# Token blocks in groups of one, two and three: a new order for attention steps and experts on one core

## The chip, the cores and the metric

The kernel runs on one core of one Trainium2 chip. The metric is device time in microseconds of that core, the median of several runs; it was 943.03 us over three runs (942.54 to 943.67).

The profile names the engines PE (matrix multiply, with its weight loads as PEld), DVE (vector), ACT (scalar activation), POOL (GpSimd) and SP (here the issuer of every DMA). Each engine takes its instructions in the order in which the program lists them, and semaphores order them across engines.

## The reference

A recurrence with a decaying state is followed by a dense mixture of four experts. Cut to what is computed:

```python
# B, H, S, D = 4, 8, 768, 48
for t in range(S):
    cur = einsum('bhd,bhe->bhde', u * k[t], v[t])
    y[t] = einsum('bhd,bhde->bhe', r[t], state + cur)
    state = w[t][..., None] * state + einsum('bhd,bhe->bhde', k[t], v[t])
x = y as (N, DM)                      # N = B*S = 3072 tokens, DM = H*D = 384
p = probs / (probs.sum(-1) + 1e-9)
for e in range(4):                    # w1[e]: 384 x 1024, w2[e]: 1024 x 384
    out += p[:, e:e+1] * (relu(x @ w1[e]) @ w2[e])
```

## The kernel before

**Units and blocks.** The sequence is cut into chunks of C = 128 steps. One batch of one chunk is an attention *unit* n (24 in all; chunk n // 4, batch n % 4). The four units of a chunk make one token *block* of 512 tokens for the experts (six blocks, 0 to 5).

**Attention.** A unit is computed in chunked form. Its parts are: `decays` (two scans on DVE that make the running decay products g and e), `scale` (r times e and k times g, on DVE), `own_product` and `own_score` (the token's own term with u: products on POOL, a reduction dg on DVE, then a diagonal a on POOL or ACT), `scores` (PE: sc, then a transpose kt; DVE copies the masked sc into a), `values` (PE: yp; ACT and DVE split it in a high part and a rest into the expert input x), `fill` (two DMAs move 16 rows of x), `carry` (PE: up; updates the state) and `guard` (ACT: tests that the decays are in range; it overwrites wx). Four steps make a unit go on: `step_a(n)` is decays(n+1) and scores(n), `step_b(n)` is scale(n+1) and own_score(n+1), `step_c(n)` is values(n), fill(n) and guard(n+1), `step_d(n)` is carry(n). `go()` takes the next step of a list; a step_c of chunk 3 or later waits in that list until an x buffer is free (three buffers). On PE a step_a shows as sc and kt, a step_c as yp, a step_d as up; step_b has no matmul.

**Experts.** For one block and one expert, a *turn*: eight f1 products (`f1`, tile pf1, two PSUM buffers; nine 128x512 matmuls each: x and w1 are split in a high part and a rest, and three products are kept), each read by ACT (relu, hh) and then by DVE (the rest, hl); then four f2 products (`f2`, tile pf2, 24 matmuls of 128x384 each, one for each batch). Weights come in quarters: `load_w` fetches a quarter into one of four raw buffers, `split_w` makes the high part on ACT and the rest with two subtractions on POOL or DVE, so eight quarters make an expert.

**Order.** All engines' lists follow the order in which the code is written. Blocks are taken in pairs: twelve passes (three pairs by four experts, the order of experts reversed from pair to pair so that one expert's weights are kept at each boundary). After each f1, and twice in each f2, `go()` takes one attention step, so a turn has 16 such gaps. In the first pass block 0 runs in two halves (SEG = 2, 2: f1 matmuls are 128x256, and each f2 has four gaps), so that it can start when two units are done. `upto(n)` takes all steps that a block needs before it starts.

**Start.** Units 0 and 1 are written out ahead of the loop, through a loop body with two rounds. `warm_up` issues matmuls on a zero tile between their parts (FILL = 12, 4, 4, 8). `setup_c` normalizes the probabilities on DVE just before the first f1.

Of the kernel before, what the change touches and what calls it, by code (L numbers as in the profile page):

```python
# [21 lines left out]
NCH = S // C  # L22
# [13 lines left out]
NRAW, XB, PB, WARM = 4, 3, 2, 12  # L36
SEG = (2, 2)
FILL = (12, 4, 4, 8)
# [3 lines left out]
def chunked_path(ctx, tc, dmaj, tmaj, u_bc, probs, w1, w2, out, flag):  # L42
# [11 lines left out]
    p_acc = pool("acc", PB)  # L54
# [122 lines left out]
    def own_score(n, diag=True):  # L177
# [4 lines left out]
        if diag:  # L182
            own_diag(n)

    def own_diag(n):
        s = un[n]
        dg = s["dg"]
# [11 lines left out]
    def decays(n):  # L199
        s = un[n]  # L200
        wx, c, b = s["wx"], s["c"], s["b"]
        g = p_one.tile([ROWS, WLEN], F32, name="g", tag="g")
        e = p_one.tile([ROWS, WLEN - 1], F32, name="e", tag="e")
        nc.vector.tensor_tensor_scan(g[:, WLEN - 1:0:-1], wx[:, WLEN - 1:0:-1], ones1[:, WLEN - 1:0:-1],  # L204
                                     0.0, ALU.mult, ALU.add)
        gv = g[:, 1:].rearrange("p (i t) -> p i t", i=NP)
# [153 lines left out]
    for sb in range(NCH // PB):  # L360
        passes += [(sb, e) for e in order]
        order = order[::-1]
    fresh = [i for i, (sb, e) in enumerate(passes) if i == 0 or passes[i - 1][1] != e]
# [71 lines left out]
    def turn(pi, e, blk, first, last, b0, nb, before, after):  # L435
        for f in range(FT):
            before(f)
            f1(e, blk, f, b0 * C, nb * C)
            after(f)
            go()  # L440
        for b in range(b0, b0 + nb):
            f2(e, blk, b, first, last, go, 4 if pi == 0 and blk == 0 else 2)

    with tc.manual_schedule():
        act_table()
        setup_a()
        for what in ("w", "k", "r"):
            load(0, what)
        nc.sync.dma_start(out=u_sb, in_=u_bc)
        for what in ("own", "v"):  # L450
            load(0, what)
        warm_up(FILL[0])
        for what in ("w", "k", "r", "own", "v"):
# [5 lines left out]
        setup_b()  # L459
        decays(0)  # L460
        guard(0)
        load(2, "w")
        scale(0)
        own_product(0)
        own_score(0)
        nc.sync.dma_start(out=pr, in_=probs)
        decays(1)
        for n in range(SEG[0]):
            scores(n)
            guard(n + 1)  # L470
            load(n + 2, "k")
            load(n + 2, "r")
            if n == 0:
                own_product(n + 1)
                own_score(n + 1, False)
            scale(n + 1)
            if n > 0:
                own_product(n + 1)
            else:
                own_diag(n + 1)  # L480
            warm_up(FILL[1])
            values(n)
            fill(n)
            if n > 0:
                own_score(n + 1)
            else:
                decays(n + 2)
            load(n + 2, "own")
            split_next((0, 1, n), n == 0)
            carry(n)  # L490
            load(n + 2, "v")
            warm_up(FILL[2])
            del un[n], steps[-4:]
            load(n + 3, "w")
        warm_up(FILL[3])
        setup_c()
        for pi, (sb, e) in enumerate(passes):
            first, last = pi % NE == 0, pi % NE == NE - 1
            for bi in range(PB):
                blk = sb * PB + bi  # L500
                next_w1 = bi == PB - 1 and pi + 1 in fresh
                own_w2 = bi == 0 and pi in fresh

                def before(f):
                    pass

                def after(f):
                    if f % 2 == 1 and next_w1:
                        split_next((passes[pi + 1][1], 1, f // 2), True)
                    if pi == 0 and bi == 0 and b0 == 0 and f % 2 == 0 and (0, 1, f // 2 + 1) in raw_t:  # L510
                        split_next((0, 1, f // 2 + 1), f % 4 == 0)
                    if f % 2 == 1 and own_w2 and b0 == 0:
                        split_next((e, 2, f // 2), pi > 0 or f % 4 == 1)
                    if f == FT - 1 and last:
                        read.add(blk)

                b0 = 0
                for nb in SEG if pi == 0 and bi == 0 else (B,):
                    if first:
                        upto(blk * B + b0 + nb - 1)  # L520
                    turn(pi, e, blk, first, last, b0, nb, before, after)
                    b0 += nb

# [189 lines left out]
```

## Time and profile before

| | us |
|---|---|
| median of three runs | 943.03 |
| the profiled execution | 942.2 |
| its span, first to last instruction | 940.4 |
| PE busy | 917.8 |
| DVE busy | 373.7 |
| POOL busy | 281.6 |
| ACT busy | 251.7 |

The profiled execution's time is 1.8 us more than its span, and 0.8 us under the median. Matmuls are pipelined and their ends are modelled, so a busy PE isn't PE at its peak: a turn's real length is read from where its first matmul starts to where the next turn's first starts. First f1 matmuls of before's turns start at 29.64 (block 0, first half), 73.71 (second half), 112.41 (block 1), 156.64 and 189.67.

### The profile page before, as it was taken

The page shows a single profiled execution, that of the slowest core. Times are in us where ns is not written, and L with a number is a line of the kernel's source. Part 1 is how long each engine was busy: PE and PEld are TensorE (multiplying, and loading weights), DVE is VectorE, ACT ScalarE, POOL GpSimd, SP SyncE. Part 2 cuts the span into 40 slices and gives each one's busy share as a digit, 9 for nine tenths or more (in the row PEclk, how much of TensorE's full clock was granted, in tenths as well). Part 3 has the DMA queues.
Part 4 walks back from the last instruction along what each step waited for, and adds up shares of the span by engine and source line. Part 5 has one row for each costly group of instructions (what it writes and reads, how often), then busy time and mean ns, then how long its engine had stood idle before and what let it go on. Part 6 is the DMA issues. An engine that isn't in the chain of part 4 may idle for free.

```text
span 940.4 us, 13744 instructions
## 1 busy us (share of the span) xinstructions
PE 917.8 (98%) x5629; PEld 818.1 (87%) x5629; DVE 373.7 (40%) x573; ACT 251.7 (27%) x454; POOL 281.6 (30%) x279
## 2 busy tenths in 40 slices
PE   6889999999999999999999999999999999999997
PEld 5778879989998978898998899898998899899887
DVE  8998793222122677742112212273202212222221
ACT  3434352231132232223213212412113312311310
POOL 5665583231132334323113213340003212311300
PEclk8999999999999999999999999999999999999999
DMA  8563542220121433331012112230102112101001
GB/s 251 173 195 119 169 151 78 68 64 22 51 68 34 143 118 117 106 93 53 32 51 68 34 34 68 61 105 10 51 1 68 35 35 68 52 33 51 9 26 37
DMA packets 34536, 70.49 MB, mean 75 GB/s; under 512 B 4512, under 2 KB 13088, under 8 KB 34464
## 3 DMA queue, kind: packets, MB, share of 16 engines
q1 hardware_dynamic: 34464, 69.52, 23.8%
q8 instruction: 46, 0.75, 0.3%
q14 instruction: 26, 0.21, 0.1%
HBM read 62.43 MB, written 4.72 MB: 71 GB/s over the span
## 4 chain that ended last, share of the span: by engine, by line
PE 91%; DVE 2%; issue 2%; DMA 1%; ACT 0%; SPq 0%; DVEq 0%
PE pf L343 42%; PE pf L323 41%; PE yp L257 2%; PE sc L230 2%; PE yp L252 2%; PE up L286 1%; DMA r<-in_dmaj 1%; PE kt L236 1%; DVE a L238 0%; DVE g L204 0%; DVE w1l L139 0%; DVE k L222 0%; DVE r L221 0%; DVE hl L330 0%; DVE zst L209 0%
## 5 line engine op out<-in xcount | busy, mean ns | idle before, releaser
L323 PE MATMUL pf<-x,w1h 128*128 128x512 f32 (+1 forms) x1200 | 362.7, 385 | 1.3 <-DMA x<-y 1.3
L330 DVE SCALAR_TENSOR_TENSOR hl<-pf,hh 128x512 fp32r<-128x512 f32 (+1 forms) x200 | 133.6, 668 | 321.8 <-ACT hh L329 321.7
L323 PEld LDWEIGHTS pf<-x,w1h 128*128 128x128 f32 x1200 | 221.0, 189 | 46.0 <-issue 2.7
L343 PE MATMUL pf<-w2h,hh 128*128 128x384 f32 x768 | 260.0, 339 | 0.0
L343 PE MATMUL pf<-w2h,hl 128*128 128x384 f32 x768 | 257.2, 335 | 0.0
L343 PE MATMUL pf<-w2l,hh 128*128 128x384 f32 x768 | 256.8, 334 | 0.0
L329 ACT ACTIVATE hh<-pf 128x512 fp32r<-128x512 f32 (+1 forms) x200 | 116.2, 581 | 459.6 <-PE pf L323 458.8
L323 PE MATMUL pf<-x,w1l 128*128 128x512 f32 (+1 forms) x600 | 229.2, 382 | 0.5 <-POOL w1l L139 0.5
L139 POOL TENSOR_TENSOR w1l<-raw,w1h 128x384 fp32r<-128x384 f32 x76 | 79.1, 1062 | 255.8 <-ACT w1h L134 255.8
L343 PEld LDWEIGHTS pf<-w2h,hh 128*128 128x128 f32 x768 | 144.2, 188 | 3.3 <-issue 1.7
L343 PEld LDWEIGHTS pf<-w2l,hh 128*128 128x128 f32 x768 | 144.2, 188 | 0.7
L343 PEld LDWEIGHTS pf<-w2h,hl 128*128 128x128 f32 x768 | 144.2, 188 | 0.3 <-DVE hl L330 0.3
L139 POOL TENSOR_TENSOR w2l<-raw,w2h 128x384 fp32r<-128x384 f32 x76 | 76.6, 1029 | 219.9 <-ACT w2h L134 217.7
L323 PEld LDWEIGHTS pf<-x,w1l 128*128 128x128 f32 x600 | 113.2, 189 | 22.5 <-POOL w1l L139 0.7
L352 DVE SCALAR_TENSOR_TENSOR acc<-pf,pr,acc 128x384 f32<-128x384 f32 x72 | 44.4, 616 | 215.6 <-PE pf L343 215.6
L195 POOL TENSOR_TENSOR a<-ident,dg 128x512 f32<-128x512 f32 x47 | 50.4, 1093 | 52.6 <-DVE dg L181 48.2
L211 DVE TENSOR_TENSOR_SCAN e<-wx,zst 112x516 f32<-112x516 f32 x24 | 50.3, 2095 | 0.8
L257 PE MATMUL yp<-a,v 128*64 128x128 f32 (+1 forms) x384 | 32.3, 296 | 11.8 <-DVE a L238 9.7
L257 PEld LDWEIGHTS yp<-a,v 128*64 128x64 f32 (+1 forms) x384 | 23.8, 138 | 18.8 <-DVE a L238 14.6
L175 POOL TENSOR_TENSOR rkt<-rkt,u_sb 128x384 f32<-128x384 f32 x22 | 37.8, 1719 | 1.7
L134 ACT CAST w1h<-raw 128x768 fp32r<-128x768 f32 x40 | 33.1, 828 | 0.0
L134 ACT CAST w2h<-raw 128x768 fp32r<-128x768 f32 x40 | 33.1, 827 | 0.0
(66 smaller groups left out, 444.1 us busy)
## 6 DMA issues: line engine op xcount, KB each, us to landing
raw<-in_w SPq DMA_DIRECT2D x80, 384.0 KB, 3.0
rkt<-in_tmaj SPq DMA_DIRECT2D x23, 384.0 KB, 3.4
wx<-in_dmaj SPq DMA_DIRECT2D x24, 226.2 KB, 3.2
k<-in_dmaj SPq DMA_DIRECT2D x24, 224.0 KB, 2.9
r<-in_dmaj SPq DMA_DIRECT2D x24, 224.0 KB, 4.0
v<-in_tmaj SPq DMA_DIRECT2D x24, 192.0 KB, 3.2
out<-acc SPq DMA_DIRECT2D x24, 192.0 KB, 1.9
x<-y SPq DMA_DIRECT2D x48, 48.0 KB, 3.0
```

The lines of the kernel that those rows point to most:

```text
L134: nc.scalar.copy(hi, t)
L139: eng.tensor_tensor(lo[:, s], t[:, s], hi[:, s].bitcast(F32), ALU.subtract)
L175: eng.tensor_tensor(s["rt"], s["rt"], u_sb, ALU.mult)
L195: nc.gpsimd.tensor_tensor(a, ident.unsqueeze(1).to_broadcast([128, NP, C]), dg[:, q].unsqueeze(2).to_broadcast([128, NP, C]), ALU.mult)
L211: nc.vector.tensor_tensor_scan(e, wx[:, 0:WLEN - 1], zst.rearrange("p i t -> p (i t)"), 0.0, ALU.mult, ALU.add)
L230: nc.tensor.matmul(sc[j][:, i, :], s["kk"][half(j), i, :], s["rr"][half(j), i, :], start=True, stop=True)
L257: nc.tensor.matmul(y[wide(j), i, :], v[:, h * D:h * D + (64 if j == 0 else D)], s["a"][j][:, i, :], start=(c == 0 and i == 0), stop=(i == ...
L323: nc.tensor.matmul(p[:, 0:nt], wv[:, k, fs], x[:, k, bs, i, :], start=(k == 0 and n == 0), stop=(k == KT - 1 and n == 2))
L329: nc.scalar.activation(hh[:, ts], p[:, 0:nt], AF.Relu)
L330: nc.vector.scalar_tensor_tensor(hl[:, ts], p[:, 0:nt], 0.0, hh[:, ts].bitcast(F32), ALU.max, ALU.subtract)
L343: nc.tensor.matmul(p, hv[:, ts], wv[:, o, :], start=(f == 0 and n == 0), stop=(f == FT - 1 and n == 2))
L352: nc.vector.scalar_tensor_tensor(a[:, b, :], p, sc, a[:, b, :], ALU.mult, ALU.add)
```

## The change

Four things change.

- **Groups.** Instead of three pairs, blocks go through the four experts as (0,), (1, 2), (3, 4, 5). There are still twelve passes and ten loads of an expert. Splits of w2 now follow the first four f1 of a pass's first turn, splits of the next expert's w1 the last four f1 of its last turn; in the group of one both fall in the same turn, eight splits in eight f1. A third `acc` buffer is added.
- **Pace.** `gap()` takes the place of `go()`: each gap adds a credit (0.5; 0.3 in the second half of block 0; 0.75 for blocks 3 to 5), and a step is taken for each full credit. In a normal turn of 16 gaps that is 8 or 12 steps, not 16.
- **Start.** Units 0 and 1 are written in another order. `decays` is cut in two, `after_decays` (g) and `until_decays` (the reciprocal and e); unit 1's g alone stands ahead of unit 0's masked copy. own_product(0) moves from DVE to POOL. r and k of unit 0 are loaded after u and the own-term rows. guard(0) moves behind scores(0), and wx of unit 2, whose buffer it frees, with it. All four w1 quarters of expert 0 are split before the first f1. The last warm-up shrinks from 4 + 8 to 4 matmuls.
- **Diagonals.** For both units 0 and 1 the second diagonal is made on ACT.

```diff
-NRAW, XB, PB, WARM = 4, 3, 2, 12
+NRAW, XB = 4, 3
+GROUPS = ((0,), (1, 2), (3, 4, 5))
 SEG = (2, 2)
-FILL = (12, 4, 4, 8)
+FILL = (12, 4, 4, 4)
...
-    p_acc = pool("acc", PB)
+    p_acc = pool("acc", max(len(g) for g in GROUPS))
...
-        eng = nc.vector if n == 0 else nc.gpsimd
-        eng.tensor_tensor(s["rt"], s["rt"], s["kt"], ALU.mult)
-        eng.tensor_tensor(s["rt"], s["rt"], u_sb, ALU.mult)
+        nc.gpsimd.tensor_tensor(s["rt"], s["rt"], s["kt"], ALU.mult)
+        nc.gpsimd.tensor_tensor(s["rt"], s["rt"], u_sb, ALU.mult)
...
-            if n == 0 and q == 1:
+            if n < SEG[0] and q == 1:
...
+    def after_decays(n):
+        s = un[n]
+        wx = s["wx"]
+        g = s["g"] = p_one.tile([ROWS, WLEN], F32, name="g", tag="g")
         nc.vector.tensor_tensor_scan(g[:, WLEN - 1:0:-1], wx[:, WLEN - 1:0:-1], ones1[:, WLEN - 1:0:-1],
                                      0.0, ALU.mult, ALU.add)
...
+    pace, credit = [0.5], [0.0]
+
+    def gap():
+        credit[0] += pace[0]
+        while credit[0] >= 1:
+            credit[0] -= 1
+            go()
...
-            before(f)
             f1(e, blk, f, b0 * C, nb * C)
             after(f)
-            go()
+            gap()
         for b in range(b0, b0 + nb):
-            f2(e, blk, b, first, last, go, 4 if pi == 0 and blk == 0 else 2)
+            f2(e, blk, b, first, last, gap, 8 // nb)
...
         decays(0)
-        guard(0)
-        load(2, "w")
-        scale(0)
         own_product(0)
+        scale(0)
         own_score(0)
-        nc.sync.dma_start(out=pr, in_=probs)
-        decays(1)
...
+        after_decays(1)
+        scores(0)
+        load(2, "k")
+        guard(0)
+        load(2, "w")
+        load(2, "own")
+        until_decays(1)
+        scale(1)
+        own_product(1)
+        warm_up(FILL[1])
+        values(0)
...
+        for blk in g:
+                segs = SEG if pi == 0 else (B,)
+                    next_w1 = blk == g[-1] and pi + 1 in fresh and b0 + nb == B
+                    own_w2 = blk == g[0] and pi in fresh and b0 == 0
+                    if pi == 0:
+                        pace[0] = 0.5 if b0 == 0 else 0.3
+                    elif blk >= GROUPS[-1][0]:
+                        pace[0] = 0.75
+                    else:
+                        pace[0] = 0.5
...
+                        if own_w2 and f < NQ:
+                            split_next((e, 2, f), pi > 0 or f % 2 == 1)
+                        if next_w1 and f >= FT - NQ:
+                            split_next((passes[pi + 1][1], 1, f - FT + NQ), True)
```

Three places show how the order moves. In the lists pf is a PSUM tile of f1, hl its second reader on DVE, and a number after a name only tells one buffer from another.

The first is DVE in a full-size turn with attention steps in its f1 phase, from the hl of the first f1 on. Before (block 1, first pass):

```order
L330 SCALAR_TENSOR_TENSOR hl<-pf_1388,hh 128x512
L204 SCALAR_TENSOR_TENSOR g<-wx,ones_100 112x516
L209 TENSOR_SCALAR zst<-g 112x4
L210 RECIPROCAL zst<-zst 112x4
L211 SCALAR_TENSOR_TENSOR e<-wx,zst 112x516
L238 COPY_PREDICATED a_1327<-mask,sc_1409 128x512
L238 COPY_PREDICATED a_1329<-mask,sc_1410 128x512
L330 SCALAR_TENSOR_TENSOR hl<-pf_1432,hh 128x512
L221 TENSOR_TENSOR r<-r,e 112x512
L222 TENSOR_TENSOR k<-k,g 112x512
L181 TENSOR_REDUCE dg<-rkt 128x8
L330 SCALAR_TENSOR_TENSOR hl<-pf_1463,hh 128x512
```

Now (block 0, second expert), the same engine and place:

```order
L334 SCALAR_TENSOR_TENSOR hl<-pf_994,hh 128x512
L203 SCALAR_TENSOR_TENSOR g<-wx,ones_100 112x516
L213 TENSOR_SCALAR zst<-g 112x4
L214 RECIPROCAL zst<-zst 112x4
L215 SCALAR_TENSOR_TENSOR e<-wx,zst 112x516
L242 COPY_PREDICATED a_874<-mask,sc_1022 128x512
L242 COPY_PREDICATED a_876<-mask,sc_1023 128x512
L334 SCALAR_TENSOR_TENSOR hl<-pf_1045,hh 128x512
L334 SCALAR_TENSOR_TENSOR hl<-pf_1066,hh 128x512
L225 TENSOR_TENSOR r<-r,e 112x512
L226 TENSOR_TENSOR k<-k,g 112x512
L183 TENSOR_REDUCE dg<-rkt 128x8
```

The hl of the second f1 stands behind the whole of step_a in both; what moved is step_b, which now comes one f1 later.

The second place is PE in the same turns, from the last matmuls of the third f1 on. Before, the yp matmuls of step_c (sixteen rows, of which the first stand here) follow the third f1, and the fourth f1 comes after them:

```order
L323 MATMUL pf_1463<-x,w1h 128x512 x2
L323 MATMUL pf_1463<-x,w1l 128x512
L252 MATMUL yp<-r,sd_112 64x128
L252 MATMUL yp<-r,sd_112 48x128
L252 MATMUL yp<-r,sd_112 64x128
```

Now the fourth f1 (pf_1097) follows at once. It takes the PSUM buffer of the second (pf_1045):

```order
L327 MATMUL pf_1066<-x,w1h 128x512 x2
L327 MATMUL pf_1066<-x,w1l 128x512
L327 MATMUL pf_1097<-x,w1h 128x512 x2
L327 MATMUL pf_1097<-x,w1l 128x512
L327 MATMUL pf_1097<-x,w1h 128x512 x2
```

The yp moved two f1 further on, behind the fifth.

The third place is DVE at the start, from the reduction of unit 0's own term (dg) on. Before:

```order
L181 TENSOR_REDUCE dg<-rkt 128x8
L204 SCALAR_TENSOR_TENSOR g<-wx,ones_100 112x516
L209 TENSOR_SCALAR zst<-g 112x4
L210 RECIPROCAL zst<-zst 112x4
L211 SCALAR_TENSOR_TENSOR e<-wx,zst 112x516
L238 COPY_PREDICATED a_192<-mask,sc_206 128x512
L238 COPY_PREDICATED a_194<-mask,sc_207 128x512
```

Now:

```order
L183 TENSOR_REDUCE dg<-rkt 128x8
L203 SCALAR_TENSOR_TENSOR g<-wx,ones_100 112x516
L242 COPY_PREDICATED a_188<-mask,sc_197 128x512
L242 COPY_PREDICATED a_190<-mask,sc_198 128x512
L213 TENSOR_SCALAR zst<-g 112x4
L214 RECIPROCAL zst<-zst 112x4
L215 SCALAR_TENSOR_TENSOR e<-wx,zst 112x516
```

The two masked copies of unit 0 moved ahead of unit 1's reciprocal and second scan.

More of the change, by code (lines that the diff above doesn't have):

```diff
@@ L172, in own_product, with own_score @@
         s = un[n]
[L173 to L177 removed]
+        nc.gpsimd.tensor_tensor(s["rt"], s["rt"], s["kt"], ALU.mult)
+        nc.gpsimd.tensor_tensor(s["rt"], s["rt"], u_sb, ALU.mult)
+    def own_score(n):
         s = un[n]
@@ L359, in chunked_path @@
     passes, order = [], list(range(NE))
-    for sb in range(NCH // PB):
-        passes += [(sb, e) for e in order]
+    for g in GROUPS:
+        passes += [(g, e) for e in order]
         order = order[::-1]
-    fresh = [i for i, (sb, e) in enumerate(passes) if i == 0 or passes[i - 1][1] != e]
+    fresh = [i for i, (g, e) in enumerate(passes) if i == 0 or passes[i - 1][1] != e]
     def step_a(n):
@@ L433, in split_next, with turn @@
         owed.append(key)
-    def turn(pi, e, blk, first, last, b0, nb, before, after):
+    pace, credit = [0.5], [0.0]
[4 more added lines that the diff above has]
+            go()
+    def turn(e, blk, first, last, b0, nb, after):
         for f in range(FT):
-            before(f)
             f1(e, blk, f, b0 * C, nb * C)
             after(f)
-            go()
+            gap()
         for b in range(b0, b0 + nb):
-            f2(e, blk, b, first, last, go, 4 if pi == 0 and blk == 0 else 2)
+            f2(e, blk, b, first, last, gap, 8 // nb)
     with tc.manual_schedule():
@@ L446, in chunked_path @@
         setup_a()
-        for what in ("w", "k", "r"):
-            load(0, what)
+        load(0, "w")
         nc.sync.dma_start(out=u_sb, in_=u_bc)
-        for what in ("own", "v"):
+        for what in ("own", "r", "k", "v"):
             load(0, what)
         warm_up(FILL[0])
-        for what in ("w", "k", "r", "own", "v"):
+        for what in ("w", "r", "k", "own", "v"):
             if what == "own":
@@ L460, in chunked_path @@
         decays(0)
+        own_product(0)
+        scale(0)
+        own_score(0)
+        after_decays(1)
+        scores(0)
+        load(2, "k")
         guard(0)
         load(2, "w")
-        scale(0)
-        own_product(0)
-        own_score(0)
-        nc.sync.dma_start(out=pr, in_=probs)
-        decays(1)
[L468 to L494, printed above, removed]
+        load(2, "own")
@@ new lines, in chunked_path @@
+        until_decays(1)
[3 more added lines that the diff above has]
+        values(0)
+        load(2, "r")
+        fill(0)
+        split_next((0, 1, 0), True)
+        own_score(1)
+        carry(0)
+        load(2, "v")
+        after_decays(2)
+        scores(1)
+        load(3, "k")
+        guard(1)
+        load(3, "w")
+        split_next((0, 1, 1), True)
+        until_decays(2)
+        warm_up(FILL[2])
+        values(1)
+        load(3, "r")
+        fill(1)
@@ L495, in chunked_path @@
+        nc.sync.dma_start(out=pr, in_=probs)
+        split_next((0, 1, 2), False)
+        own_product(2)
+        scale(2)
+        carry(1)
+        load(3, "v")
+        split_next((0, 1, 3), True)
+        own_score(2)
+        load(3, "own")
+        guard(2)
+        load(4, "w")
         warm_up(FILL[3])
+        del un[0], un[1], steps[-8:]
         setup_c()
-        for pi, (sb, e) in enumerate(passes):
+        for pi, (g, e) in enumerate(passes):
             first, last = pi % NE == 0, pi % NE == NE - 1
[L499 to L515, printed above, removed]
-                b0 = 0
-                for nb in SEG if pi == 0 and bi == 0 else (B,):
@@ L519, in chunked_path @@
                     if first:
                         upto(blk * B + b0 + nb - 1)
-                    turn(pi, e, blk, first, last, b0, nb, before, after)
+                    turn(e, blk, first, last, b0, nb, after)
                     b0 += nb
```

17 lines of the change are left out of this document (9 added, 8 removed).

## The prediction

> **What bounds the kernel now.** I read the page first, then the span by stages, then the start and one turn in order of time.
>
> ```profile
> span 940.4 us, 13744 instructions
> PE 917.8 (98%) x5629; PEld 818.1 (87%) x5629; DVE 373.7 (40%) x573; ACT 251.7 (27%) x454; POOL 281.6 (30%) x279
> PE   6889999999999999999999999999999999999997
> DVE  8998793222122677742112212273202212222221
> PE 91%; DVE 2%; issue 2%; DMA 1%; ACT 0%; SPq 0%; DVEq 0%
> PE pf L343 42%; PE pf L323 41%; PE yp L257 2%; PE sc L230 2%; PE yp L252 2%; PE up L286 1%; DMA r<-in_dmaj 1%; PE kt L236 1%; DVE a L238 0%; DVE g L204 0%; DVE w1l L139 0%; DVE k L222 0%; DVE r L221 0%; DVE hl L330 0%; DVE zst L209 0%
> ```
>
> PE carries the chain (91%). It has holes only in the first slices of 23.5 us, where DVE is at eight to nine tenths; later PE is full whatever DVE does, and where DVE works hard (attention) its order must be such that PE never waits for it. By stages (columns: PE, PEld, DVE, ACT, POOL busy, clock, DMA share, GB/s):
>
> ```profile
> 29.64:73.71 44.07, 38.20 (x361) 32.57 (x361) 41.22 (x64) 18.11 (x40) 30.00 (x26) 0.92 0.59 182
> 73.71:112.41 38.70, 37.02 (x395) 31.75 (x393) 34.01 (x56) 14.28 (x35) 21.14 (x21) 1.00 0.47 142
> 156.64:189.67 33.03, 33.03 (x170) 30.18 (x169) 7.38 (x11) 8.26 (x13) 7.93 (x8) 1.00 0.14 48
> 333.34:385.28 51.94, 51.94 (x443) 43.72 (x441) 38.03 (x61) 15.27 (x32) 21.38 (x21) 1.00 0.41 123
> ```
>
> A bare turn takes 33.03 us; by the chain's 42% (L343) half of it, 16.5, is f2. The turn at 333.34 holds four attention units: (51.94 - 33.03) / 4 = 4.73 us of PE time a unit, with no hole. The two halves of block 0's first turn hold four units each and take 82.77 us. A half f1 is nine matmuls, three in 0.36 us:
>
> ```profile
> 33.14 0.40 PE L323 MATMUL pf<-x,w1h 128*128 128x256 f32 x2
> 33.50 0.40 PE L323 MATMUL pf<-x,w1h 128*128 128x256 f32 x2
> ```
>
> So 1.08, and 16 x 1.08 + 16.5 and eight units at 4.73 make 71.6: 11 us of PE time are lost there, and 29.64 pass before it. All that the change can win lies in these 41 us; the matmuls that remain are the same, apart from twelve warm-ups.
>
> **The start.** Rows of before in order of time:
>
> ```profile
> 6.66 0.72 ACT L297 ACTIVATE wx<-wx,mid 112x512 f32<-112x512 f32 x1 [4.36 <-DVE e L211]
> 7.21 0.68 DVE L222 TENSOR_TENSOR k<-k,g 112x512 f32<-112x512 f32 x1
> 10.43 0.33 SPq L153 DMA_DIRECT2D wx<-in_dmaj  x1
> 13.10 1.32 DVE L238 COPY_PREDICATED a<-mask,sc 128x512 f32<-128x512 uint32 x2
> 18.44 1.40 DVE L204 TENSOR_TENSOR_SCAN g<-wx,ones 112x516 f32<-112x516 f32 x1
> 22.61 1.30 DVE L238 COPY_PREDICATED a<-mask,sc 128x512 f32<-128x512 uint32 x2
> 25.33 3.02 PE L105 MATMUL pf<-zero 128*128 128x512 f32 x12
> 25.97 0.55 DVE L267 TENSOR_TENSOR x<-yp,x 112x384 fp32r<-112x384 f32 x1
> 26.58 1.20 SPq L274 DMA_DIRECT2D x<-y  x2
> 29.64 0.47 PE L323 MATMUL pf<-x,w1h 128*128 128x256 f32 x2 [1.29 <-DMA x<-y]
> ```
>
> DVE is the path: copy of unit 0 at 13.10, of unit 1 at 22.61, x done at 26.52, and 3.1 us later (two DMAs) f1. Unit 0: r and k come later (u and the own rows go first, 0.58 MB, some 2 us at this stage's rate), so I put the end of scale(0) at 8.6, not 7.89. The product on POOL gives the diagonal at about 11, and since e of unit 1 (2.3 us with its reciprocal) no longer stands ahead, the copy comes at 11.2, 1.9 earlier. Unit 1: its copy loses its predecessor's e too (18.44 + 1.40 to 22.61 is 2.8), but g of unit 2 must still run first, and its wx is requested later: guard(0), at 6.66 before, now stands behind the diagonals and ks on ACT and ends near 12.9, so this DMA goes out 2.5 us later and SP holds what is queued behind it (own rows, r, the fill). I put its landing at 18.7, the copy at 20.0, x at 24.0 and the first f1 at 27.1: 2.5 us won. Bounds: 25 (wx lands as before) and 29.
>
> The warm-ups at the end were twelve of 0.25; with four PE idles from about 24.0 to 27.1. What that does to the clock:
>
> ```profile
> 19.84:23.25 3.41, 2.17 (x20) 1.00 0.68 218
> 26.66:30.08 3.42, 2.13 (x12) 1.00 0.38 102
> 33.50:36.91 3.41, 1.46 (x13) 1.00 0.60 184
> 36.91:40.32 3.41, 3.32 (x21) 0.50 0.02 5
> ```
>
> (PE busy, clock, DMA.) A window of 3.41 us with 2.13 or 2.17 us of work leaves the next at full clock; one with 1.46 is followed by a window at half. So f1 will start at half clock, 1.5 us lost. It stays hidden: DVE still has a split, scale(2), dg and setup_c to do until about 29.5 and sets the pace.
>
> **First half of block 0.** Before, the f1 phase stalls like this:
>
> ```profile
> 35.88 1.31 DVE L238 COPY_PREDICATED a<-mask,sc 128x512 f32<-128x512 uint32 x2
> 36.69 2.50 PE L257 MATMUL yp<-a,v 128*64 128x128 f32 x16 [1.95 <-ACT w1h L134]
> 37.09 0.40 DVE L330 SCALAR_TENSOR_TENSOR hl<-pf,hh 128x256 fp32r<-128x256 f32 x1
> ```
>
> PE waits 1.95 for the copy, and hl, which must free a PSUM buffer, comes after it. Half a quarter's split on DVE, by the groups of lines:
>
> ```profile
> L139 DVE TENSOR_TENSOR w2l<-raw,w2h 128x384 fp32r<-128x384 f32 x4 | 2.0, 548 | 0.3 <-ACT w2h L134 0.3
> ```
>
> The new order keeps one unit instead of two in these eight f1, with step_a behind the second. DVE from 29.5: hl (0.4), a w2 quarter (2 x 0.55), hl, decays(3) with two copies (6.0, between the 5.19 and 6.60 of rows below), hl: 37.8. The fifth f1 waits for that hl; PE was done at about 34.3 (27.1, four f1, sc and kt, half clock), 3.5 us lost. Then split, hl, scale(3), dg and two hl put the seventh at 43.2 and the end of f1 at 46.0. f2 with unit 3: 8.3 + 3.7 (4.73 without the state product, the 1.08 of L252 below) = 58.0. The second half needs x of unit 3, whose yp is only two gaps before: yp ends 54.9, x 56.6, DMAs 3.1: 59.7, 1.7 lost (before, those units were done long ahead). Second half: 8.6 + 8.3 of matmuls, unit 4 with 4.7, a like stall of 3.0 (5.2 to 6.6 of DVE and 0.8 of hh and hl against two f1 and sc with kt, 3.7), ends 84.3; one half-clock window, 1.7, makes 86.0. Before stands at 112.41 with ten units; now five are done, and 112.41 - 5 x 4.73 = 88.8. **Term: -2.8**, bounds -7 (f1 at 25, stalls as short as the 1.95) and +1 (f1 at 29, DVE beside a busy POOL).
>
> **The pace.** Moved units cost 4.73 as before where nothing waits; grouping itself adds no matmul and no load (twelve passes, ten experts either way), the third acc buffer nothing. In a full-size turn before:
>
> ```profile
> 114.67 1.16 PE L230 MATMUL sc<-r,k 48*128 48x128 f32 x16
> 115.40 0.69 DVE L330 SCALAR_TENSOR_TENSOR hl<-pf,hh 128x512 fp32r<-128x512 f32 x1 [2.52 <-ACT hh L329]
> 116.01 1.22 DVE L204 TENSOR_TENSOR_SCAN g<-wx,ones 112x516 f32<-112x516 f32 x1
> 119.87 1.33 DVE L238 COPY_PREDICATED a<-mask,sc 128x512 f32<-128x512 uint32 x2
> 120.41 1.08 PE L252 MATMUL yp<-r,sd 48*64 48x128 f32 x16
> 121.09 0.67 DVE L330 SCALAR_TENSOR_TENSOR hl<-pf,hh 128x512 fp32r<-128x512 f32 x1
> 122.44 0.73 PE L323 MATMUL pf<-x,w1h 128*128 128x512 f32 x2
> ```
>
> After sc, PE runs two f1 until 120.41. The second-next hl on DVE (121.09) stands behind decays and copies and ends at 121.76; it frees the buffer of the fourth f1. Before, yp fills 120.41 to 122.44, so nobody waits. Now, at half a step a gap, the fourth f1 comes straight after the third and must wait from 120.41 to 121.76: **1.35 us** a unit. The order shows eight full-size f1 phases with a step_a, decays behind it and three f1 in a row: the turns of experts 2, 3 and 4 on block 0, both blocks of the pass after, block 1 of the next, block 2 in that group's last, and block 3's first. In four of these (the three on block 0, and block 1's second pass) POOL splits w2 quarters in the same f1. What that does to DVE:
>
> ```profile
> 139.15 2.89 POOL L139 TENSOR_TENSOR w1l<-raw,w1h 128x384 fp32r<-128x384 f32 x2
> 139.23 2.02 DVE L204 TENSOR_TENSOR_SCAN g<-wx,ones 112x516 f32<-112x516 f32 x1
> 144.50 1.33 DVE L238 COPY_PREDICATED a<-mask,sc 128x512 f32<-128x512 uint32 x2
> ```
>
> From g to the last copy 6.60 instead of 5.19, so the wait would be 2.76. POOL starts later against g here (after ACT's cast), so I take the middle of 1.35 and 2.76, 2.05. Terms: 4 x 1.35 = **+5.4**, 4 x 2.05 = **+8.2** (bounds 5.4 and 11.0).
>
> A hole of 2.05 can leave a 3.41 us window with 1.36 of work, under the 1.46 that was followed by half clock; where the window's edge cuts the hole it won't. Half of the four: 2 x 1.7 = **+3.4** (bounds 0 and 6 x 1.7 = 10). A step_a in an f2 phase needs no hl and costs nothing. Eight splits in one turn are up to 8 x 2.89 = 23 us of POOL, beside a unit's own work, in an f1 phase of some 22: POOL ends late, but each half's next use is an f1 or f2 phase away, 16.5 us, so nothing.
>
> The Trainium skill, "TensorE: Matmul & The Clock Gate", under "Why this matters for your kernels", says that PE falls back to half rate after an idle gap of more than about 3 us, one idle window. By that rule no hole of 2.76 throttles and the sum would lack the 3.4. The trace disagrees: 33.50:36.91 had 1.46 us of work, and the next window ran at 0.50; the case without half clocks is a rival below, worked out from rows.
>
> **Sum**, against the profiled execution (942.2): -2.8 + 5.4 + 8.2 + 3.4 = +14.2, 956.4. The median of the runs is 0.8 above that execution: 957.
>
> **Rivals.**
> - *Faster.* The start and the first half are worth more than I give, and the fourth f1 does not wait. For it: 13 us of holes and 29.64 of start are there, and half the DVE load of the first f1 phase goes. Point of decision: the eight waits must come to under 2.8 us, 0.35 each; or the start must gain 14. With no wait 942.2 - 2.8 = 939.4, at the best start 935: 936 to 940 on the median's scale. Against it: hl stands behind the copies in the list, and the copy's end is in the rows. Chance 0.13.
> - *No half clock* in the holes: 957.2 - 3.4 = 953.8. For it: 2.13 us of work was enough. Against: 1.46 wasn't. Chance 0.25.
> - *The weights come late.* In the group of one a raw buffer is asked for again only when POOL is done with it, SP holds later loads behind that request, and an ACT cast that waits holds relu. With 3 us and a half-clock window in each of three turns: 957 + 3 x 4.7 = 971. Against: POOL's lag is about 3 us and each quarter is asked for three splits ahead. Chance 0.10.
> - *About as before*, where start and waits cancel: 0.05, 941 to 945.
>
> My forecast proper, with two to six half windows: 0.47, its own range 948 to 965. Within 0.2% (941.1 to 944.9) is about what a measurement of this kernel can tell from no change. Faster 0.13, same 0.05, slower 0.82. Leaving out the faster case and half of the late weights: 943 to 968.
>
> **What would show it.** First f1 near 27 with a half-clock window there; copies of units 0 and 1 near 11 and 20; a hole before the fifth half f1; the second half's first f1 waiting for the DMA of x; in the turns of block 0 a PE wait of 1.4 to 2.8 at the fourth f1 after each sc, released by hl, with the clock line below 9 somewhere between 100 and 300; bare turns still 33.03. I am wrong if PE shows no wait there, or if f1 starts before 25.

## The result and the profile after

The changed kernel takes 955.88 us (median of four runs, 955.75 to 955.96), the kernel before took 943.07 beside it on the same chip. The ratio is 1.0136 with a 95% interval of 1.0118 to 1.0153: slower by 12.8 us, where 957.0 was forecast. The profiled execution has a span of 954.2, before's had 940.4: 13.8 us more.

The first lines of the page of the changed kernel, and its chain by engine:

```profile
span 954.2 us, 13657 instructions
...
PE 917.4 (96%) x5617; PEld 815.8 (85%) x5617; DVE 377.0 (40%) x569; ACT 253.6 (27%) x458; POOL 293.4 (31%) x282
...
PE   6698999999999999999999999999999999999997
...
PE 90%; DVE 4%; issue 3%; DMA 1%; ACT 1%; SPq 0%; POOL 0%; DVEq 0%
```

PE has the same busy time as before (917.4 against 917.8), so the lost time is idle time of PE. DVE's share of the chain has doubled (2% to 4%), with one and the same load (377.0 against 373.7). The digit 9 hides all of this: a tenth of a slice is 2.4 us. What PE waited for says it (engine, line, what released it; total, times, longest), first up to 110 us, then from there to 960:

```profile
PE pf L327 <- DVE hl L334: 7.0, 4, 2.7
...
PE pf L327 <- DMA pr<-in_probs: 4.3, 1, 4.3
PE pf L327 <- DMA x<-y: 2.1, 1, 2.1
```
```profile
PE pf L327 <- DVE hl L334: 9.1, 7, 1.7
```

The 4.3 and the 2.1 are the first f1 of the two halves, which wait for x. The first is put down to the load of the probabilities, which no f1 reads; it stands right behind the two DMAs of x in the queue. After 110 us one kind of wait is left in the whole kernel, seven times: an f1 (pf) that waits for an hl. An eighth stands at 99.03, in the first full turn. Its place, in order of time:

```profile
91.74 1.16 PE L234 MATMUL sc<-r,k 48*128 48x128 f32 x16
...
93.09 1.22 DVE L203 TENSOR_TENSOR_SCAN g<-wx,ones 112x516 f32<-112x516 f32 x1
...
94.34 0.80 DVE L213 TENSOR_SCALAR zst<-g 112x4 f32<-112x4 f32 x1
...
95.40 1.78 DVE L215 TENSOR_TENSOR_SCAN e<-wx,zst 112x516 f32<-112x516 f32 x1
...
97.10 1.30 DVE L242 COPY_PREDICATED a<-mask,sc 128x512 f32<-128x512 uint32 x2
...
98.31 1.27 DVE L334 SCALAR_TENSOR_TENSOR hl<-pf,hh 128x512 fp32r<-128x512 f32 x2
...
99.03 0.73 PE L327 MATMUL pf<-x,w1h 128*128 128x512 f32 x2 [1.48 <-DVE hl L334]
...
103.33 1.08 PE L256 MATMUL yp<-r,sd 48*64 48x128 f32 x16
```

This is the forecast hole: decays and copies on DVE, two hl behind them, and the fourth f1 of the turn waiting 1.48 us for the first of the two; yp, which covered the place before, now comes at 103.33. By stages (columns as in the prediction):

```profile
30.83:63.50 32.67, 27.61 (x225) 25.13 (x225) 23.58 (x40) 12.77 (x28) 18.59 (x16) 0.90 0.54 164
63.50:89.57 26.07, 23.59 (x189) 22.18 (x190) 12.38 (x20) 9.02 (x19) 13.93 (x13) 0.93 0.42 123
89.57:133.80 44.23, 42.75 (x306) 36.84 (x305) 25.04 (x35) 16.40 (x29) 29.06 (x26) 1.00 0.44 138
350.70:383.73 33.03, 33.03 (x170) 30.18 (x170) 8.00 (x12) 7.68 (x12) 7.96 (x8) 1.00 0.16 48
```

With five units done, the changed kernel stands at 89.57; before stands at 88.8 by the prediction's count: 0.8 lost in the early part. From there to the end it takes 954.2 - 89.57 = 864.6, before 828.0 (940.4 - 112.41) and five units of 4.73, 851.6: 13.0 lost in the later part. A bare turn is still 33.03.

### The profile page after: what moved, and what is told of

Its sections match the earlier page's. It is cut to its first block, busy times and chain, and to the rows that moved or that the text cites. A ratio compares the mean times of both kernels' runs of the same rounds, so it can differ in the third digit from the quotient of the medians.

```text
span 954.2 us, 13657 instructions
## 1 busy us (share of the span) xinstructions
PE 917.4 (96%) x5617; PEld 815.8 (85%) x5617; DVE 377.0 (40%) x569; ACT 253.6 (27%) x458; POOL 293.4 (31%) x282
## 4 chain that ended last, share of the span: by engine, by line
PE 90%; DVE 4%; issue 3%; DMA 1%; ACT 1%; SPq 0%; POOL 0%; DVEq 0%
PE pf L347 42%; PE pf L327 39%; PE yp L261 3%; PE yp L256 2%; PE sc L234 2%; DVE a L242 1%; PE up L290 1%; PE kt L240 1%; DVE g L203 1%; DVE hl L334 1%; DMA k<-in_dmaj 1%; ACT hh L333 0%; DMA pr<-in_probs 0%; DMA x<-y 0%; DVE e L215 0%
## 5 line engine op out<-in xcount | busy, mean ns | idle before, releaser
L327 PE MATMUL pf<-x,w1h 128*128 128x512 f32 (+1 forms) x1200 | 366.4, 388 | 22.4 <-DVE hl L334 16.1
L142 POOL TENSOR_TENSOR w1l<-raw,w1h 128x384 fp32r<-128x384 f32 x78 | 82.5, 1082 | 242.9 <-ACT w1h L137 242.1
L142 POOL TENSOR_TENSOR w2l<-raw,w2h 128x384 fp32r<-128x384 f32 x76 | 84.0, 1128 | 135.6 <-ACT w2h L137 134.9
L191 POOL TENSOR_TENSOR a<-ident,dg 128x512 f32<-128x512 f32 x46 | 47.9, 1062 | 43.4 <-DVE dg L183 33.1
L220 POOL TENSOR_TENSOR sd<-st,g 112x192 f32<-112x192 f32 x20 | 16.8, 838 | 137.0 <-DVE g L203 137.0
L215 DVE TENSOR_TENSOR_SCAN e<-wx,zst 112x516 f32<-112x516 f32 x24 | 47.0, 1958 | 0.8
L234 PEld LDWEIGHTS sc<-r,k 48*128 48x128 f32 x384 | 24.2, 193 | 13.5 <-DVE k L226 7.2
L234 PE MATMUL sc<-r,k 48*128 48x128 f32 x384 | 29.0, 292 | 6.3 <-DVE k L226 6.3
L177 POOL TENSOR_TENSOR rkt<-rkt,u_sb 128x384 f32<-128x384 f32 x23 | 33.8, 1469 | 1.8
```

The costliest lines, as they stand in the source:

```text
L142: eng.tensor_tensor(lo[:, s], t[:, s], hi[:, s].bitcast(F32), ALU.subtract)
L177: nc.gpsimd.tensor_tensor(s["rt"], s["rt"], u_sb, ALU.mult)
L215: nc.vector.tensor_tensor_scan(e, wx[:, 0:WLEN - 1], zst.rearrange("p i t -> p (i t)"), 0.0, ALU.mult, ALU.add)
L234: nc.tensor.matmul(sc[j][:, i, :], s["kk"][half(j), i, :], s["rr"][half(j), i, :], start=True, stop=True)
L327: nc.tensor.matmul(p[:, 0:nt], wv[:, k, fs], x[:, k, bs, i, :], start=(k == 0 and n == 0), stop=(k == KT - 1 and n == 2))
```

## The experiments

The time given for each run is its median, and the ratio is to the kernel before, measured beside it on the same chip. Before's own median there lay between 943.07 and 943.91, so times of runs that were not measured together compare only to about 1 us.

**Is it the pace?** *A step in every gap after block 0's first turn; all else as changed:*

```diff
-                    elif blk >= GROUPS[-1][0]:
-                        pace[0] = 0.75
                     else:
-                        pace[0] = 0.5
+                        pace[0] = 1.0
```

> The changed kernel with a full credit a gap in every turn after block 0's first (pace 1 instead of 0.5 and 0.75); groups, start and first turn stay. Theory 1 (the loss is PE waiting at the fourth f1 for an hl that stands behind step_a on DVE): yp comes back between the third and the fourth f1, the eight waits of 11.9 us go: 944.0, between 942.5 and 945.5, and no PE wait on hl after 90 us. Theory 2 (the loss is the group of one with eight splits in a turn, or the first halves): it stays above 952.

944.14 us, ratio 1.0012 (1.0000 to 1.0024). Of the waits for hl after 90 us 0.4 us are left, in two places, and from the first full turn (90.96) to the end it takes 851.64, which is before's 851.6. So the later loss goes with the pace, and the groups of one, two and three cost and win nothing there.

*Two units a turn as changed (now for blocks 3 to 5 too, which made three), but all steps in f2 gaps once block 0's first turn is over:*

```diff
-    def gap():
+    def gap(f1_phase=False):
+        if f1_phase and pace[0] == 1.0:
+            return
         credit[0] += pace[0]
...
-            gap()
+            gap(True)
...
-                    elif blk >= GROUPS[-1][0]:
-                        pace[0] = 0.75
                     else:
-                        pace[0] = 0.5
+                        pace[0] = 1.0
```

> The changed kernel with its halves of block 0 as they are, and afterwards steps in f2 gaps alone (one in each, so still two units a turn). Theory (the eight waits are the whole loss of the later turns): first f1 at 29 to 31, halves 32.7 and 26.1, so the full turns begin near 89, take 42.45 each with two units, and from there to the end 851 to 852: span 940.5, time 942, range 940.5 to 943.5. Rival (something else in the pace, such as late weights or more DVE work beside f1, costs time too): 945 or more.

942.17 us, ratio 0.9987 (0.9979 to 0.9996). This is the cleanest run: as many units in each turn of blocks 0 to 2, as much DVE work (376.1 us against 377.0), and another place for it. One full turn of it (131.55) by the windows:

```profile
131.55:174.00 42.45, 42.45 (x306) 37.08 (x305) 24.13 (x37) 15.82 (x28) 27.55 (x26) 1.00 0.45 140
```

PE is busy for all 42.45 us, where the changed kernel's turn took 44.23 with 42.75 busy; DVE does 24.13 against 25.04. PE waits for nothing from 90 us on. DVE was never too slow, it was busy at the wrong moment. The rival (late weights, or DVE's load as such) is out for the full turns.

*The same from the start, halves of block 0 included* (no gap in an f1 phase takes a step; a full step in every f2 gap):

> The changed kernel with every attention step moved into the f2 phases: a gap in an f1 phase takes nothing, a gap in an f2 phase takes a step, so each turn still makes two units and no hl stands behind step_a. Theory (the loss is the fourth f1 waiting for an hl behind decays and copies, and a step_a in an f2 phase costs nothing): the eight waits (11.9 us) and the stalls in the two halves (2.85 and 2.64) go, full turns with two units take 42.5; the last x of the first half comes late, so its wait grows from 2.1 to about 3.5: 955.9 - 11.9 - 5.5 + 1.4 = about 940, range 937 to 942. Rival (DVE is simply too slow for a unit at this pace, wherever it stands): the wait moves to yp, or to the release of the f2 buffers, and full turns stay at 44: 950 or more.

942.51 us, ratio 0.9992 (0.9983 to 1.0001): full turns of 42.45 again, but 2.5 us over the forecast. The halves did not win what I gave them. Waits of PE from 30 us to the end:

```profile
PE pf L327 <- DMA wx<-in_dmaj: 3.8, 1, 3.8
PE pf L327 <- DVE hl L334: 2.2, 2, 1.9
```

The first stands at the start of the second half, as in the changed kernel, and has grown from 2.1 to 3.8: unit 3's x is made only in the last f2 (the load that is named stands behind the DMAs of x in the queue). The hl of the first f1 phase still waits in two places.

**Which part of step_a?** *decays cut: g in step_a, reciprocal and e at the head of step_b; pace as changed:*

```diff
     def step_a(n):
         if n + 1 < NU:
-            decays(n + 1)
+            after_decays(n + 1)
...
     def step_b(n):
         if n + 1 < NU:
+            until_decays(n + 1)
             scale(n + 1)
```

> The changed kernel, but decays(n+1) cut in the steps too: g in step_a, the reciprocal and e in step_b. The pace stays 0.5 and 0.75. Theory 1: hl of the second f1 now stands behind 2.6 us of DVE work instead of 5.2, so the fourth f1 finds its buffer free; the halves of block 0 lose less as well (2.9 and 2.6 us there); a new wait of up to 0.4 may come two f1 after step_b. 942 to 947. If the wait comes from the pace itself and not from the length of DVE's work ahead of hl, or from POOL's splits: 953 or more.

946.6 us, ratio 1.0036 (1.0023 to 1.0048). Turns without splits fall to 42.5, those of block 0 only to 43.95, for there the hole has moved behind step_b:

```profile
97.14 3.34 POOL L142 TENSOR_TENSOR w2l<-raw,w2h 128x384 fp32r<-128x384 f32 x2
...
98.30 1.31 DVE L225 TENSOR_TENSOR r<-r,e 112x512 f32<-112x512 f32 x1
...
99.54 1.49 DVE L226 TENSOR_TENSOR k<-k,g 112x512 f32<-112x512 f32 x1
...
101.41 1.27 DVE L334 SCALAR_TENSOR_TENSOR hl<-pf,hh 128x512 fp32r<-128x512 f32 x2
...
102.14 0.73 PE L327 MATMUL pf<-x,w1h 128*128 128x512 f32 x2 [1.42 <-DVE hl L334]
```

The scaling of r and k takes 1.31 and 1.49 beside POOL's split; the shortest rows of both in before's trace have 0.67. The second half of block 0 took 21.93 instead of 26.07: its stall is gone. The first half, at 34.42, is no shorter.

*Both edits, the cut and a step in every gap after the first turn:*

> The changed kernel with two edits: decays cut in its two parts (g in step_a, the rest in step_b), and a step in every gap after block 0's first turn. Theory: the start and the halves take what they took with the cut alone (first f1 30.3, halves 34.4 and 21.9, 86.6 in all), the rest what it took at full pace (851.6, no wait): span 938.2, time 940, range 939 to 942. Rival (at full pace the cut puts a wait in front of the f1 that follows step_b): 945 or more.

944.35 us, ratio 1.0013 (1.0002 to 1.0025): outside both ranges, and nearer the rival's. The halves end at 86.18 as expected, but the two turns of four units take 54.09 and 51.36 instead of 52.04 and 49.20. The largest wait of PE from 86 to 200 us, of a kind that the run without the cut does not have there:

```profile
PE yp L261 <- DVE a L242: 2.2, 4, 0.9
```

The rival's kind of wait, at an f1 for its hl, adds 1.4 us there; the larger part stands at yp, for the masked copies. The two turns lose 4.2 us; that the heavier step_b makes the copies late is the likely reason, not a tested one.

**The start.** *Before's start (order, loads, warm-ups, early splits) in front of the changed loop*; the edit takes over the lines of before from the loads of unit 0 to setup_c, own_product, own_score, FILL and its places of the first w1 and w2 splits:

> The old start (units 0 and 1 as before, 12 + 4 + 4 + 4 + 4 + 8 warm-ups, the last two w1 quarters split in the first f1) with the new groups and pace. If the new start costs what the two traces show (first f1 at 30.8 instead of 29.6): 954.7, the eight waits unchanged. If the new start is a gain that its own first f1 does not show (four quarters split ahead, so less work on DVE and ACT in the first half): 956 to 959.

957.36 us, ratio 1.0160 (1.0139 to 1.0182); first f1 at 30.85, halves 33.45 and 24.55.

*The changed start, then before's pairs, split places and pace:*

```diff
-GROUPS = ((0,), (1, 2), (3, 4, 5))
+GROUPS = ((0, 1), (2, 3), (4, 5))
...
-                    if pi == 0:
-                        pace[0] = 0.5 if b0 == 0 else 0.3
...
+                    pace[0] = 1.0
```

> The new start with the old pairs, the old places of the splits and a step in every gap. If start and the rest add up: 943.1 + 1.2 = 944.3, first f1 at 30.8, no wait on hl after the first turn. If the new start relieves the first half (less split work there): 940 to 943.

942.32 us, ratio 0.9990 (0.9980 to 1.0000); first f1 at 30.03. Both runs point to a gain of 1 to 1.5 us by the new start, but at the edge of the noise: this interval reaches 1.0000, and that of the run with before's start overlaps the changed kernel's (1.0118 to 1.0153).

*The fill first: three loads of unit 3 and one weight quarter moved behind the two DMAs that fill unit 1's x:*

```diff
-        load(3, "k")
         guard(1)
-        load(3, "w")
-        split_next((0, 1, 1), True)
+        split_w((0, 1, 1), True)
+        owed.append((0, 1, 1))
...
-        load(3, "r")
         fill(1)
+        load(3, "k")
+        load(3, "w")
+        more_raw()
+        load(3, "r")
```

> The changed kernel with only the order of SP's queue at the start changed: the loads of k, wx and r of unit 3 and of the third w2 quarter come behind the two fill DMAs of unit 1. Theory (the fill stands behind those loads, and lands 3.3 to 3.7 us after its issue instead of 2.2): the first f1 comes 1 to 1.5 us earlier, 29.5, and the time falls as much: 954.6, range 954 to 955.4. Rival (DVE and POOL, not the queue, hold the first f1, or DVE's list sets the pace of the first half anyway): 955.9, no change.

957.00 us, ratio 1.0145 (1.0131 to 1.0160): no gain. The first f1 did come 1.75 us earlier, at 29.08, and the half lasted 5 us longer (37.69):

```profile
34.64 0.25 DVE L117 TENSOR_REDUCE prs<-pr 128x24 f32<-128x96 f32 x1 [3.27 <-DMA pr<-in_probs]
...
44.31 0.80 PE L327 MATMUL pf<-x,w1h 128*128 128x256 f32 x2 [4.77 <-DVE hl L334]
```

The probabilities now come behind those loads, and DVE waits 3.27 us for them with the hl of the first f1 queued behind. The 1.75 us need not be the edit's either: other executions with the loads where they were began f1 as early as 28.87 (below). Three executions with the changed kernel's halves took 34.1 to 35.7 for this one (also below), so only 2 to 3.6 of the 5 us are out of the ordinary. I tried the order once more without that wait, in the fastest kernel.

**The groups alone.** *A step in every gap everywhere, halves included:* `pace[0] = 1.0` in place of all four values.

> The changed kernel with a step in every gap everywhere, halves included: the new start and the groups of one, two and three are left, the pace is not. Theory (grouping costs nothing, the pace is the whole loss): as the run with the new start and the old pairs, 942.3, range 941 to 944. Rival (eight splits in one turn of the group of one, beside a unit's work, delay weights or DVE): three turns of 3 us more, 951 or above.

946.16 us, ratio 1.0036 (1.0023 to 1.0049): between the two forecasts, and 3.8 over the run with the same start and pairs. The difference is in one place, block 0's second half: 42.08 us here, 38.68 there. The first line is that half with groups, the second, of the other kernel, with pairs:

```profile
74.04:116.12 42.08, 38.55 (x394) 32.98 (x392) 38.20 (x56) 17.09 (x39) 32.48 (x28) 0.96 0.56 167
```
```profile
74.44:113.12 38.68, 37.02 (x394) 31.74 (x392) 33.98 (x56) 14.29 (x35) 21.32 (x21) 1.00 0.48 144
```

In the group of one the next expert's w1 splits fall into this half: POOL does 32.48 us instead of 21.32, and DVE needs 38.20 instead of 33.98 for the same 56 instructions. PE's waits in it for the masked copies grow from 1.6 to 3.5 us, and one window of 3.41 us runs at half clock (the half's mean is 0.96). With four units in it, DVE sets the pace there. So grouping costs nothing only where few units share a turn with splits; at the changed kernel's pace it cost nothing.

**The half clock.** *Copies into an unused tile added on DVE behind the masked copies of six units, to lengthen the holes:*

```diff
+HOLE = {5: 1, 7: 2, 9: 3, 11: 4, 13: 9, 15: 6}
...
         scores(n)
+        for i in range(HOLE.get(n, 0)):
+            nc.vector.tensor_copy(junk, ones1[:, 0:256])
```

> The changed kernel with copies into an unused tile added on DVE behind the masked copies of units 5, 7, 9, 11, 13 and 15 (1, 2, 3, 4, 9 and 6 copies of 112x256, about 0.25 us each): the holes at the fourth f1 grow from 1.6 (0.5 for unit 13) to about 1.9, 2.2, 2.4, 2.5, 2.8 and 3.1. It leaves nothing out. Theory (a 3.41 us window with less than about 1.5 us of PE work is followed by one at half clock, so a hole of 2 or more throttles unless a window's edge cuts it): one half-clock window or more after the holes of 2.4 to 3.1, 2 to 4 of the six, each 1.7 us: 955.9 + 6.2 + 3.4 to 6.8, so 965 to 969. Rival (PE falls back only after a hole of more than about 3 us): no half clock, or one: 962 to 964.

975.87 us, ratio 1.0342 (1.0324 to 1.0360), beyond both forecasts: a copy takes 0.54 us in the mean, not 0.25 (0.3 to 0.4 in the two places where POOL is mostly idle, 0.7 to 0.9 in the three where its products and splits run beside them). The six holes came out at 1.71, 2.77, 3.77, 2.52, 3.83 and 6.77 (24.4 us of waits for hl after 80 us, against 10.6), and after the last four of them a window at half clock follows. Two of them, the first matmul behind each, and the profiler's 3.41 us windows at these two, each with the next (PE busy first, clock third from the right):

```profile
142.92 0.73 PE L329 MATMUL pf<-x,w1h 128*128 128x512 f32 x2 [2.77 <-DVE hl L336]
...
236.13 0.73 PE L329 MATMUL pf<-x,w1h 128*128 128x512 f32 x2 [2.52 <-DVE hl L336]
```
```profile
141.20:144.62 3.42, 1.70 (x7) 1.42 (x8) 3.39 (x5) 0.30 (x1) 3.42 (x4) 1.00 0.00 0
144.62:148.03 3.41, 3.41 (x26) 2.66 (x26) 2.56 (x5) 1.99 (x4) 3.41 (x4) 1.00 0.53 142
233.35:236.77 3.42, 0.90 (x5) 0.55 (x4) 3.32 (x9) 0.60 (x1) 0.54 (x1) 1.00 0.00 0
236.77:240.18 3.41, 3.41 (x10) 2.64 (x9) 1.56 (x3) 0.33 (x1) 1.70 (x2) 0.50 0.23 53
```

The hole of 2.77 lies across a window's edge, leaves 1.70 us of work in one window and isn't followed by half clock. The shorter one of 2.52 lies inside a window, leaves 0.90, and is. In this pair the work left in the window decides, not the length of the hole. The changed kernel at the same place, the window with its hole and the next one:

```profile
96.08:99.49 3.41, 1.93 (x9) 1.31 (x8) 3.41 (x5) 2.11 (x4) 3.33 (x5) 1.00 0.38 115
99.49:102.90 3.41, 3.41 (x17) 2.80 (x16) 3.41 (x5) 1.32 (x2) 3.41 (x4) 1.00 0.02 6
```

Its holes after 90 us leave 1.90 or more, and full clock follows every time. Before's row of 1.46 was followed by 0.50. The edge between them isn't sharp in PE's busy time. A window of the run with the groups alone had 1.80 us of work and was still followed by half clock:

```profile
100.89:104.30 3.41, 1.80 (x18) 1.37 (x19) 3.41 (x5) 0.26 (x2) 3.41 (x4) 1.00 0.78 215
104.30:107.71 3.41, 3.41 (x25) 2.88 (x24) 2.52 (x4) 2.29 (x6) 2.67 (x4) 0.50 0.10 38
```

Over all traces of this case, from 15 us on, a window at full clock with up to 1.55 us of work was always followed by half clock, one with 1.85 or more never, and between 1.66 and 1.84 both came. The rule of the Trainium skill that the prediction weighed ("TensorE: Matmul & The Clock Gate", "Why this matters for your kernels": half rate after an idle gap of more than about 3 us) gives the right answer for the full turns of the changed kernel. It does not for the hole of 2.52, nor for one of 2.69 in the changed kernel's first half (at 41.16, below), which a window at half clock follows as well.

**The best of both.** *Steps in f2 gaps after block 0's first turn, and decays cut while that turn runs:*

```diff
     def step_a(n):
         if n + 1 < NU:
-            decays(n + 1)
+            after_decays(n + 1)
+            un[n + 1]["cut"] = pace[0] < 1
+            if not un[n + 1]["cut"]:
+                until_decays(n + 1)
...
     def step_b(n):
         if n + 1 < NU:
+            if un[n + 1]["cut"]:
+                until_decays(n + 1)
             scale(n + 1)
```

> The same with decays cut in its two parts while block 0's halves run, whole afterwards. Theory: the halves take what they took with the cut (34.4 or 34.9, and 21.9), the full turns begin at 86.4, the rest takes 851.5: span 938, time 939.5, range 938.5 to 941, under both kernels. Rival (the cut only moves DVE's lateness on to the first full turn): as without the cut, 942.

940.16 us, ratio 0.9963 (0.9950 to 0.9976): the fastest, 3.5 us under the 943.62 of before beside it. Its halves take 35.28 and 23.30; the full turns begin at 87.45, and the rest takes 850.9 (938.4 - 87.45), with no wait.

*The same with the fill first again, but one weight quarter left ahead and setup_c moved behind the fifth f1:*

```diff
-        load(3, "k")
         guard(1)
-        load(3, "w")
         split_next((0, 1, 1), True)
...
-        load(3, "r")
         fill(1)
+        for what in ("w", "k", "r"):
+            load(3, what)
...
-        setup_c()
...
+                        if pi == 0 and b0 == 0 and f == 4:
+                            setup_c()
```

> The fastest kernel so far (cut decays in the halves, steps in f2 gaps afterwards; 940.16) with the start's queue changed as in the run with the fill first, but without that run's new wait: the loads of k, wx and r of unit 3 come behind the fill of unit 1, the third w2 quarter keeps its place ahead of it, and setup_c moves from ahead of the first f1 to behind the fifth, so that DVE no longer waits there for the probabilities. Theory (the fill is late because of the loads ahead of it on SP, and the run with the fill first lost it again only by DVE's wait for the probabilities, 3.3 us): first f1 0.5 to 1.5 us earlier, at about 28, the first half no longer than 35.3, time 939 to 939.7. Rival (DVE's own list sets the end of the first half, whenever f1 starts): the half grows by what the start wins: 940.2, within 0.5.

943.32 us, ratio 0.9985 (0.9975 to 0.9994): 3.2 slower than without. The fill was issued at 26.66 and f1 began at 29.68, 3.02 later; without the edit it was 25.73 and 28.87, 3.14. So the loads ahead of the fill did not delay it in the fastest kernel's execution, and f1 began 0.81 later because the fill was issued later. The larger loss lies in the half, 37.67 instead of 35.28: setup_c is DVE work ahead of an hl wherever it stands. The time is above both expectations. What PE waits for most from 26 to 100 us:

```profile
PE pf L327 <- DVE hl L334: 5.5, 4, 3.2
```

Without the edit it is 4.0 in three waits. The rest of the 2.4 is not traced.

## Why the prediction came out right, step by step

The sum was +14.2, and the span grew by 13.8. Two terms were wrong by some 3.5 us each, and cancelled: the early part came out at +0.8 instead of -2.8, the half clock at 0 instead of +3.4. That the total agrees to 0.4 us is luck; that eight waits for hl cost over 10 us is not.

- **The pace: mechanism and turns right, price nearly.** There are eight waits, one in each of the eight turns that were named, and all are for an hl behind step_a; moving the steps removes all eight. Six stand at the fourth f1, the other two at the eighth (508.08) and the sixth (548.11). By the waits they are 1.48 and 9.1, 10.6 us, against 13.6 forecast. But each costs some 0.3 more than its wait shows (a turn takes 44.23 against 42.45 without the hole, 1.78 for 1.48 of waiting), so that the later part lost 13.0. What those 0.3 are was not looked into, and they make up for most of what the waits lack.
- **The price beside POOL's splits was the mis-sized one:** 2.05 forecast, 1.48 measured in each of the four, hardly more than in three without splits (1.32 to 1.67). The bare price already held POOL: in a turn without splits e takes 2.26 beside POOL's products of the next unit, in the turn above zst takes 0.80 and e 1.78 beside the split. From g to the last copy that is 5.17 and 5.31. I had put the one on top of the other. In the last of the eight places (274.71) no product of POOL falls beside e, which takes 1.29, and the wait is 0.38. The bare place of the changed kernel:

```profile
225.79 1.22 DVE L203 TENSOR_TENSOR_SCAN g<-wx,ones 112x516 f32<-112x516 f32 x1
...
227.47 2.26 DVE L215 TENSOR_TENSOR_SCAN e<-wx,zst 112x516 f32<-112x516 f32 x1
...
227.62 1.01 POOL L176 TENSOR_TENSOR rkt<-rkt 128x384 f32<-128x384 f32 x1
...
229.65 1.31 DVE L242 COPY_PREDICATED a<-mask,sc 128x512 f32<-128x512 uint32 x2
...
231.58 0.73 PE L327 MATMUL pf<-x,w1h 128*128 128x512 f32 x2 [1.33 <-DVE hl L334]
```

- **Half clock in the holes: +3.4 forecast, none came.** The mechanism exists, as the lengthened holes show, but holes of 1.5 leave 1.9 us of work. The rival "no half clock" (953.8) was right on this term. Had the contended price been 2.05, as forecast, a window could have fallen to 1.36.
- **The start: the step that failed.** 27.1 was forecast for the first f1, 30.83 came, and DVE's first hl came at 33.22 instead of about 29.5. Rows of the changed kernel:

```profile
12.35 1.35 DVE L242 COPY_PREDICATED a<-mask,sc 128x512 f32<-128x512 uint32 x2 [0.87 <-POOL a L191]
...
14.25 0.33 SPq L156 DMA_DIRECT2D wx<-in_dmaj  x1
...
20.10 1.99 DVE L203 TENSOR_TENSOR_SCAN g<-wx,ones 112x516 f32<-112x516 f32 x1 [0.21 <-DMA wx<-in_dmaj]
...
22.02 1.31 DVE L242 COPY_PREDICATED a<-mask,sc 128x512 f32<-128x512 uint32 x2
...
25.61 0.42 SPq L160 DMA_DIRECT2D r<-in_dmaj  x1
...
26.58 1.20 SPq L278 DMA_DIRECT2D x<-y  x2
...
33.22 0.43 DVE L334 SCALAR_TENSOR_TENSOR hl<-pf,hh 128x256 fp32r<-128x256 f32 x1
```

  Unit 0's copy waits for the diagonal from POOL (12.35, not 11.2); wx of unit 2, asked for at 14.25, lets g start only at 20.10, and g takes 1.99; so unit 1's copy comes at 22.02, not 20.0, and x is done at 26.52, to the hundredth as before. From the fill's issue to the first f1 it then took 4.25 in this execution and 2.9 to 3.15 in all the others. The queue says what differed, by the median time from issue to landing of the DMAs issued near 26 us:

```profile
r<-in_dmaj SPq DMA_DIRECT2D x1, 224.0 KB, 4.5
x<-y SPq DMA_DIRECT2D x2, 48.0 KB, 3.5
```

  The load of unit 3's r went out 0.97 us ahead of the fill and landed at 30.1, and the fill landed after it. In the nine other executions of this start that load went out 1.58 us or more ahead. So the fill most likely queued behind it here; no run tests that alone. Those ten executions (some with changed loops) began f1 between 28.87 and 30.83, 29.7 in the mean; before's start gave 29.64 and 30.85 in two. So of the 2.5 the new order won about half a microsecond, as far as so few executions show.
- **The halves: the sums right, by luck in part.** 32.67 and 26.07 were measured, 32.6 and 26.3 forecast; the wait before the second half was 2.1 (1.7). The stalls for hl were shorter than forecast (2.7 and 0.3 against 3.5 in the first half, 2.5 against 3.0 in the second), and the first half had two windows at half clock, not one. More telling, the late first f1 cost nothing. The run with a step in every gap after block 0's first turn has the same code up to the end of the halves. It began f1 at 29.20, and its fifth f1 came no earlier. The changed kernel, then that run:

```profile
41.16 0.57 PE L327 MATMUL pf<-x,w1h 128*128 128x256 f32 x2 [2.69 <-DVE hl L334]
```
```profile
41.14 0.50 PE L327 MATMUL pf<-x,w1h 128*128 128x256 f32 x2 [3.06 <-DVE hl L334]
```

  Two more runs share these halves, the one with all steps in f2 gaps afterwards and the one with lengthened holes; f1 began at 29.44 and 29.08. In these three the first half took 34.1 to 35.7 us, and the second half began between 63.2 and 64.9, against 63.50 here. So DVE's list, through its hl, sets the first half's pace, and not the first f1. The forecast had DVE done with the third hl at 37.8; it was done at 41.11, 3.3 later, and most of the +0.8 instead of -2.8 is that. The +0.8 is a draw as well: in these three the full turns begin at 90.96, 89.20 and 87.71, so that the same count gives +2.2, +0.4 and -1.1. None comes to -2.8.

## What to carry to other kernels

An instruction on a lightly loaded engine that frees a buffer of the bound engine is a deadline: look at what stands ahead of it in that engine's list, and at which work covers the wait. If that cover (here yp behind the third f1) is moved, the old wait appears, though loads and counts are the same. Put heavy side work where no such deadline lies, here in the f2 phases; even pacing by itself does not do that. And moving the first start of the bound engine helps only if the engine that frees its buffers is ahead as well: here f1 at 29.20 and at 30.83 led to the same fifth f1.

## What the runs showed of the hardware

- The same DVE instruction, beside a POOL operation over two SBUF tiles and without one: zst 0.80 and 0.17, e 2.26 and 1.23, r times e 1.31 to 1.55 and 0.68. The Trainium skill ("SBUF — State Buffer", "Who interferes with whom") says that a DVE instruction with two inputs in SBUF contends with a GpSimd one that reads SBUF; the last two of these agree.
- A 3.41 us window at full clock with 1.55 us of PE work or less was followed by half clock, one with 1.85 or more never, and between 1.66 and 1.84 both were seen; a hole of 2.52 throttled where one of 2.77 did not.
- A DVE copy of 112x256 from one SBUF tile took 0.3 to 0.4 us where POOL was mostly idle (behind units 11 and 13 of the run with lengthened holes), and 0.7 to 0.9 beside its products and splits (units 7, 9 and 15).
- The same start code began its first f1 within 28.87 to 30.83 us from run to run.
